# Two loads of v moved from SyncE's DMA queue to ScalarE's, in a sparse-attention and maxout kernel

## The chip, the cores and the metric

One core of one Trainium2 chip. The metric is the device time of one execution in microseconds. The kernel before has a median of 173.41 us (172.84, 173.2 and 173.63, and one slow run of 175.87).

## The reference

```python
batch, n_heads, seq, head_dim = 4, 8, 768, 64        # q, k, v in float32
block, window = 32, 16
k_sum = k.reshape(B, H, nb, block, D).max(axis=3)     # block maxima of k
v_sum = v.reshape(B, H, nb, block, D).mean(axis=3)    # block means of v
# each query sees its window of 2*16-1 keys, and all 24 block maxima (+ log 32)
a = softmax(concat(window scores, block scores))
attn = a @ concat(v, v_sum)
x = attn as (3072, 512)
out = maximum(x @ w1, x @ w2) @ w_out                 # d_ff = 1024
```

The kernel computes the maximum as w1-part plus relu of x times wd, with wd = w2 - w1. The first attention needs k and q of batch 0, then v of batch 0 (two loads of four heads, called the first and the second v below), and the first hidden product needs x of that attention and wd.

## The kernel before: the parts concerned

Each engine's instruction order, and the landing slot of each load, are fixed by a list (S is SyncE, A ScalarE, D VectorE, G GpSimd, P TensorE; the number is the task, the digit behind the colon a slot).

```python
ORDER = (
    "D3 S38:0,0 D6:0 S40:1,0 D1 D0 ... A92:0 S13:0 G5:0 A101:1 "
    "S14:4 P103:0,0 A93:2 ... A96:1,0 G32:0,0 S41:0 D68:3 D11:0 P70:4,0 S16:5 "   # S14, S16: the two loads of v of batch 0
    "D97:0 P95:0 A77:1 D72:0,0 S42:6 ... S43:7 D83 D84 P88:2 D106:1 S52:0 "      # S42.. : weights
    "P90:6 A89:0 D15:0,0 P86:4 A91:1 D19 ... D17:0 ...")                         # D15, D17: casts of v
# ... cut ...
land = Ring(tiles("land", 8, [128, 2048], F32))       # eight landing slots for all loads

def load_v(b, prio, gap, on):
    vb, parts = Buf(vbr), [Buf(Ring([None])) for _ in range(2)]
    # ... cut ...
    for n in range(2):
        f = Buf(land)
        view = lambda f=f: f.ap[:, 0:1536].rearrange("p (h m d) -> p h m d", h=4, d=D)
        op("SP", 3.6, lambda view=view, n=n: nc.sync.dma_start(
            out=view().rearrange("p h m d -> p (h m) d"),
            in_=v[b, 4 * n:4 * n + 4].rearrange("h (m r) d -> r (h m) d", r=128)),   # rows of 64 floats = 256 B
           write=[f], behind=v_spread[b - 1], prio=prio + gap * n, label=f"load v{b}{n}")
        copy(on, ...)                                  # the cast of v, on VectorE for b = 0
# ... cut ...
def split_w12(n, fs, prio, prio_t):
    part = slice(256 * (n % 2), 256 * (n % 2) + 256)
    op("DVE", {"DVE": 1.2, "POOL": 2.36}, lambda e: (nc.vector if e == "DVE" else nc.gpsimd).tensor_tensor(
        out=wd[n].ap[:], in0=wide(fs[1])[:, :, part], in1=wide(fs[0])[:, :, part], op=ALU.subtract), ...)
```

The softmax here doesn't subtract the row's maximum and nothing guards it: scores larger than these inputs give would overflow.

## Time and profile before

| | before |
|---|---|
| median, us | 173.41 |
| profiled span, us | 171.9 |
| first hidden matmul (TensorE, line 660) starts, us | 30.74 |
| from there to the end, us | 141.2 |
| VectorE casts the first v / the second v at, us | 16.93 / 20.98 |

The page's main rows and SyncE's issues stand in the prediction. First ScalarE's timeline at the place where the second v will be issued (start us, duration us, engine, line, operation, tiles, and in brackets the idle time before it with what ended it):

```profile
9.25 0.79 ACT L410 COPY kx<-banks 128x768 bf16<-128x768 bf16 x1
10.65 0.83 ACT L410 CAST kqb<-land 128x768 bf16<-128x768 f32 x1 [0.61 <-DMA land<-in_k_dram]
12.08 0.80 ACT L410 COPY kx<-banks 128x768 bf16<-128x768 bf16 x1 [0.60 <-PE banks L434]
```

The last of these, ScalarE's second kx copy, is read by VectorE's third block maximum of k (the "third reduction" below):

```profile
13.91 0.95 DVE L454 TENSOR_REDUCE ks<-kx 128x24 bf16<-128x768 bf16 x1
```

Then GpSimd's and VectorE's timelines between 22 and 31 us:

```profile
23.77 1.20 POOL L410 CAST w1b<-land 128x1024 bf16<-128x1024 f32 x1 [10.06 <-DMA land<-in_moe_w_dram]
26.52 4.86 POOL L607 TENSOR_TENSOR wd<-land,land 128x1024 bf16<-128x1024 f32 x2 [1.55 <-DMA land<-in_moe_w_dram]
```

### The profile page before, as it was taken

Reading aid. Unit: us, or ns where it says so; the run is one execution under the profiler, and the core shown is the slowest. Engines: PE = TensorE matmul, PEld = TensorE weight load, DVE = VectorE, ACT = ScalarE, POOL = GpSimd, SP = SyncE. Lnnn points to the kernel's source line nnn. Section 1 sums busy time; section 2 is a strip of 40 time slices with the busy share of each in tenths; the row PEclk is TensorE's granted clock in tenths of the full one; section 3 lists DMA queues with packets and bytes.
Section 4 is the critical chain, followed back from the end, with each engine's and each line's share of the span. In section 5 each row is a group of like instructions: output and inputs, shape, how many; then the busy total and the mean of one; then the engine's idle time right before and its main releaser. Section 6 shows DMA issues by size and latency. Waiting matters only on the chain.

```text
span 171.9 us, 5167 instructions
## 1 busy us (share of the span) xinstructions
PE 148.1 (86%) x2229; PEld 97.5 (57%) x2256; DVE 114.6 (67%) x208; ACT 89.3 (52%) x120; POOL 41.5 (24%) x61
## 2 busy tenths in 40 slices
PE   0136585999999999899999989999999999999992
PEld 0124354645865575468656745677565558856451
DVE  1279999847767869759898847799896741224031
ACT  3375897756865795348768252567553140231020
POOL 7521028522263002795003375100000000000000
PEclk9999969999999999999999999999999999999999
DMA  4999999999999799999999955720022110000645
GB/s 159 341 293 221 305 388 386 391 373 338 221 281 251 154 270 235 253 312 350 323 263 158 256 169 98 229 77 4 0 89 98 65 61 0 4 0 0 208 158 183
DMA packets 42742, 34.22 MB, mean 199 GB/s; under 512 B 25952, under 2 KB 36704, under 8 KB 42720
## 3 DMA queue, kind: packets, MB, share of 16 engines
q1 hardware_dynamic: 42720, 33.90, 70.0%
q8 instruction: 17, 0.28, 0.7%
q14 instruction: 5, 0.04, 0.1%
HBM read 25.17 MB, written 6.29 MB: 183 GB/s over the span
## 4 chain that ended last, share of the span: by engine, by line
PE 78%; DVE 11%; DMA 4%; issue 2%; ACT 1%; SPq 1%; DVEq 0%
PE banks L660 24%; PE banks L681 24%; PE banks L674 11%; DVE vx L410 4%; PE banks L501 4%; DMA land<-in_k_dram 4%; PE banks L644 4%; PE banks L543 4%; PE banks L434 3%; PE banks L575 2%; DVE ks L454 2%; DVE qx L410 1%; SPq L305 1%; PE banks L346 1%; DVE xs L552 1%
## 5 line engine op out<-in xcount | busy, mean ns | idle before, releaser
L660 PE MATMUL banks<-xt,wd 128*128 128x256 bf16 x384 | 46.6, 273 | 0.0
L681 PE MATMUL banks<-wo,g 128*128 128x512 bf16 (+1 forms) x187 | 44.1, 370 | 1.6 <-issue 1.4
L660 PEld LDWEIGHTS <-wd 128*128 128x128 bf16 x384 | 36.8, 98 | 8.5
L515 ACT ACTIVATE pb<-banks,bias 128x1024 bf16<-128x1024 f32 x24 | 25.8, 1113 | 7.7 <-PE banks L501 7.6
L406 ACT ACTIVATE g<-banks 128x512 bf16<-128x512 f32 x30 | 17.2, 599 | 22.9 <-PE banks L660 22.7
L681 PEld LDWEIGHTS <-g 128*128 128x128 bf16 x200 | 18.3, 98 | 17.0
L410 POOL CAST kqb<-land 128x768 bf16<-128x768 f32 x18 | 16.0, 904 | 42.6 <-DMA land<-in_q_dram 20.2
L674 PE MATMUL banks<-w1o,xt 128*128 128x512 bf16 (+1 forms) x88 | 23.1, 370 | 1.2 <-issue 0.8
L408 DVE TENSOR_SCALAR g<-banks 128x512 bf16<-128x512 f32 x18 | 12.3, 689 | 13.8 <-PE banks L660 13.6
L410 ACT COPY o<-banks 128x512 f32<-128x512 f32 (+1 forms) x15 | 8.6, 571 | 22.8 <-PE banks L681 22.6
L434 PE MATMUL banks<-identity,kqb 64*128 64x64 bf16 x384 | 9.9, 201 | 11.7 <-ACT kqb L410 6.7
L552 DVE TENSOR_TENSOR xs<-banks,inv 128x512 bf16<-128x512 f32 x24 | 16.1, 684 | 0.5
L434 PEld LDWEIGHTS <-kqb 64*128 64x128 bf16 x384 | 7.7, 101 | 15.0 <-ACT kqb L410 6.8
L454 DVE TENSOR_REDUCE ks<-kx 128x24 bf16<-128x768 bf16 x16 | 15.0, 944 | 1.4 <-ACT kx L410 1.2
L674 PEld LDWEIGHTS <-xt 128*128 128x128 bf16 x100 | 9.1, 98 | 7.9
L410 DVE COPY o<-banks 128x512 f32<-128x512 f32 (+1 forms) x10 | 6.6, 663 | 10.3 <-PE banks L681 8.3
L509 DVE TENSOR_TENSOR pb<-pb,mask 128x1024 bf16<-128x1024 bf16 x18 | 13.2, 750 | 0.3 <-ACT pb L515 0.2
L410 ACT COPY qx<-banks 128x768 bf16<-128x768 bf16 x12 | 9.5, 804 | 5.6 <-PE banks L434 2.8
L501 PEld LDWEIGHTS <-kx 64*128 64x128 bf16 x416 | 8.6, 102 | 5.4 <-issue 3.9
L501 PE MATMUL banks<-qx,kx 64*128 64x64 bf16 (+2 forms) x416 | 10.2, 199 | 1.0 <-DVE kx L461 0.5
L543 PEld LDWEIGHTS <-pb 128*64 128x64 bf16 x384 | 7.5, 110 | 6.1 <-issue 4.3
L410 DVE COPY kx<-banks 128x768 bf16<-128x768 bf16 x7 | 6.7, 952 | 6.5 <-PE banks L434 5.5
(63 smaller groups left out, 149.6 us busy)
## 6 DMA issues: line engine op xcount, KB each, us to landing
land<-in_k_dram SPq DMA_DIRECT2D x16, 384.0 KB, 6.9
land<-in_q_dram SPq DMA_DIRECT2D x16, 384.0 KB, 8.2
land<-in_v_dram SPq DMA_DIRECT2D x8, 768.0 KB, 10.4
out_dram<-o SPq DMA_DIRECT2D x19, 256.0 KB, 2.5
land<-in_moe_w_dram SPq DMA_DIRECT2D x4, 1024.0 KB, 10.4
land<-in_moe_w_out_dram SPq DMA_DIRECT2D x2, 1024.0 KB, 14.3
vx<-vb SPq DMA_DIRECT2D x3, 396.0 KB, 7.1
out_dram<-o SPq DMA_DIRECT2D x4, 224.0 KB, 3.4
```

What stands on the lines that cost most here:

```text
L406: nc.scalar.activation(out=o, in_=i, func=ACT.Relu)
L410: {"DVE": nc.vector.tensor_copy, "ACT": nc.scalar.copy, "POOL": nc.gpsimd.tensor_copy, "SP": nc.sync.dma_start}[e](out=o, in_=i)
L434: nc.tensor.transpose(out=bank(ps, 2048, BF16)[:, at:at + 64], in_=src.ap[r, j].rearrange("p h d -> p (h d)"), identity=identity[r, r])
L454: op("DVE", 0.95, lambda: nc.vector.tensor_reduce(out=ks.ap[:].rearrange("p (t s) -> p t s", s=2), in_=kt()[:, :, 0:64].rearrange("p t (s ...
L501: nc.tensor.matmul(**m)
L509: nc.vector.tensor_tensor(out=o, in0=o, in1=m, op=ALU.mult)
L515: op("ACT", 1.13, lambda: nc.scalar.activation(out=pb.ap[:].rearrange("p a n -> p (a n)"), in_=bank(ps, 1024), func=ACT.Exp, bias=bias[:], ...
L543: nc.tensor.matmul(out=av()[64 * par:64 * par + 64, c, 2 * u + a, :], lhsT=pb.ap[:, a, at:at + 64], rhs=vx[b].ap[:, 4 * grp + 2 * u + par, ...
L552: op("DVE", 0.69, lambda: nc.vector.tensor_tensor(out=x.ap[:, grp] if g1 == grp else x.ap[:, grp:g1 + 1, hp % 2], in0=av()[:, :, :, 0:D], ...
L660: nc.tensor.matmul(out=bank(ps)[:, 256 * s:256 * s + 256], lhsT=wd[n].ap[:, c, 128 * s:128 * s + 128], rhs=x_rows(b, grp)[:, c, :], start= ...
L674: nc.tensor.matmul(out=bank(ps, hi - lo), lhsT=x_rows(b, grp)[:, c, sl], rhs=w1o[c].ap[:, lo:hi], start=(c == 0), stop=False)
L681: nc.tensor.matmul(out=bank(ps, hi - lo), lhsT=g.ap[:, f, sl], rhs=wo[f // 2].ap[:, f % 2, lo:hi], start=False, stop=(f == FC - 1))
```

## The change

The intent: with v on a second queue, the q load behind it no longer sits 8.54 us in its issue, weights can be issued earlier, and v travels beside k, q and the weights.

```diff
-            op("SP", 3.6, lambda view=view, n=n: nc.sync.dma_start(
+            op("SP", 3.6, lambda view=view, n=n: (nc.sync if b else nc.scalar).dma_start(
                 out=view().rearrange("p h m d -> p (h m) d"),
                 in_=v[b, 4 * n:4 * n + 4].rearrange("h (m r) d -> r (h m) d", r=128)),
```

## The prediction

> **What bounds the kernel now.** I read the page first. Its 40 slices say that TensorE is busy at 90% or more from the eighth slice on (some 30 us into a span of 171.9 us), and that the DMA engines are full over the same first 30 us:
>
> ```profile
> span 171.9 us, 5167 instructions
> ...
> PE   0136585999999999899999989999999999999992
> ...
> DVE  1279999847767869759898847799896741224031
> ...
> DMA  4999999999999799999999955720022110000645
> ```
>
> So there are two stretches: a start of 30 us in which loads and VectorE prepare the first attention, and 140 us in which TensorE is packed. The chain that ended last, in order of time, agrees: one k load up to 9.53 us, then almost nothing but VectorE pieces to 30 us, then TensorE pieces to the end. A microsecond lost before 30 us therefore moves the end by about a microsecond; there is no later slack to swallow it. One gained counts only if it shortens that VectorE stretch.
>
> Second, the timeline of the start, SyncE's DMA issues (start, duration, what):
>
> ```profile
> 0.82 0.96 SPq L305 DMA_DIRECT2D land<-in_k_dram  x2
> 1.81 0.47 SPq L305 DMA_DIRECT2D land<-in_q_dram  x1
> 2.33 0.98 SPq L305 DMA_DIRECT2D land<-in_k_dram  x2
> 3.35 0.99 SPq L305 DMA_DIRECT2D land<-in_q_dram  x2
> 4.38 0.47 SPq L327 DMA_DIRECT2D land<-in_v_dram  x1
> 4.89 8.54 SPq L305 DMA_DIRECT2D land<-in_q_dram  x1
> ...
> 13.48 0.47 SPq L327 DMA_DIRECT2D land<-in_v_dram  x1
> ```
>
> The q load after the first v sits in its issue for 8.54 us. That is what the change is after. But the queue is not empty meanwhile. The trace's landings (last of 16 parts): first q 8.49 us, third and fourth k 9.51 and 10.57, next q's 11.61 and 12.74, first v 15.42, the blocked q 16.51, second v 19.96, w1 23.72. The engines carry the earlier loads until v is through, with about 1 us of thinner traffic near 13 to 14 us.
>
> Third, what VectorE does with them:
>
> ```profile
> 9.53 0.56 DVE L410 CAST kqb<-land 128x768 bf16<-128x768 f32 x1 [1.90 <-DMA land<-in_k_dram]
> ...
> 16.06 0.95 DVE L454 TENSOR_REDUCE ks<-kx 128x24 bf16<-128x768 bf16 x1
> 16.93 0.95 DVE L410 CAST vb<-land 128x1536 bf16<-128x1536 f32 x1
> 17.98 0.57 DVE L410 COPY vx<-vb 64x1584 bf16<-64x1584 bf16 x1
> 18.58 0.56 DVE L410 CAST kqb<-land 128x768 bf16<-128x768 f32 x1
> ...
> 20.98 0.96 DVE L410 CAST vb<-land 128x1536 bf16<-128x1536 f32 x1
> ```
>
> Only the k cast waits for a DMA, 1.90 us. The v casts start with no wait: VectorE arrives 1.5 us after the first v landed (16.93 against 15.42) and 1.0 us after the second (20.98 against 19.96). In windows of 4.3 us VectorE is busy 4.12, 4.08, 4.21 and 4.07 us from 12.9 to 30. An earlier v is worth nothing there; a v that is over 1 to 1.5 us later, or a later k, costs.
>
> **What the Trainium skill says.** "DMA: Bandwidth & Descriptors", section Issuing engines are not separate DMA queues: the transfers of all issuers run on the same 16 engines and interleave, and a second issuer "will only save the time on the sequencer it takes to initiate the DMA, which is usually small relative to the DMA itself". The trace agrees on one shared resource (full from 2 to 37 us), but here one issue lasts 8.54 us. The same page, Queues, rings and completion order: each DMA engine round-robins between queues at packet granularity, and SP and ACT have a ring of their own on each engine but no descriptor generator of their own. The trace before has one data queue, so it shows nothing of the sharing. It does show that every row of v is a packet of 256 B (3072 a load, 192 per engine), against 1536 B for k and q (16 per engine and load) and 2048 B for the weights (32).
>
> **The change part by part.** The built program shows what moves: TensorE, VectorE and GpSimd keep their order. ScalarE gets the first v behind its second cast (5.24 us) and the second v behind its first kx copy (9.25 us). SyncE loses two issues, and the wo load that followed the third weight load now also waits for the first v to land, through a shared semaphore.
>
> Removed: 8.54 us of SyncE blocking. The last q comes out about a microsecond sooner than 16.51, but VectorE casts it only at 18.58. The weights move ahead of v. Weights are first needed at 23.8 us, and the first hidden matmul at 30.7 waits for VectorE's x, which waits for v. Gain on the path: about 0, at most the 1 us of thin traffic.
>
> Added, first: the share of v. The trace's windows give rates over 16 engines: 352 to 372 GB/s with 1536 B packets, 228 to 239 with 256 B, 388 with 2048 B. Per engine one packet takes 66, 17.5 and 84 ns. If the two queues take turns packet by packet, v gets one small packet per big one: 84 ns a turn beside k and q, 102 ns beside weights, where alone it would take 17.5. First v packets flow about 1.1 us after the issue (0.82 to 1.9 for the first k), so near 6.5 us. I count on the slowest engine, since a load has landed only when it has (first q: 15 parts by 6.2 us, the last at 8.49). At 7.4 us it has six k and q loads left, 96 packets: 96 x 84 ns = 8.1 us, to 15.5. Half of v's 192 packets are through. The other 96 pair with the three weight loads already queued: 96 x 102 ns = 9.8 us, to about 25.3. The first v lands near 25.5 instead of 15.42, and VectorE loses 25.5 - 16.9 = 8.6 us. The second v then runs alone until wo is released (4 us, to 29) or shares with wo and the next weights (up to 40): 8 to 19 us behind its 20.98. These losses overlap, as both are waits of one in-order engine: 8 to 19 us in all.
>
> Added, second: k and q slow down. The third k, the one VectorE waits for, has 32 packets ahead and in it: 32 x 17.5 ns = 0.6 us later, straight on the chain; the fourth 0.8.
>
> Added, third: ScalarE can be blocked as SyncE was. The issue behind a v was accepted about 2 us before that v's last part landed (13.43 against 15.42; 17.38 against 19.96; in the next batch 44.47 against 47.02), so with some 100 packets of v left on the slowest engine. With turns of 84 ns, about 92 packets are gone at 7.4 + 7.7 = 15.1 us. ScalarE would hang in the second v's issue from 9.3 to 15 us, and its k cast (10.65), kx copy and qx copies start 4 to 5 us late. That delay lies inside the wait for v.
>
> Sum in full: 173.2 + 8 to 19, less a little overlap, so 180 to 191.
>
> **The rivals.** (a) Sharing by bytes, not packets: v gets half the rate, some 16 small packets for every 2.7 of k and q. Then v lands before 15 us and ScalarE is hardly held, but the third k is pushed back by up to 3 us, and the whole VectorE chain with it: 174 to 177. For it: the skill's remark that a packet can hold several descriptors. Against: the trace records every 256 B row by itself. (b) The shared generator holds everything behind a full ScalarE ring: the first v still pairs with what is queued, to 20 to 24 us, but the second then has the engines to itself, about 4 us: 178 to 182. (c) Nothing moves: v hardly competes, lands in its 1 to 1.5 us of slack, and VectorE's stretch stays: 173 to 174. For it speaks only that the bytes and the consumers' order are unchanged. (d) Faster: the thin microsecond is saved and small packets hide under big ones, 172 to 173. It can't become 2%, because VectorE is full from 9.5 us on and the first k loads are ahead of v in either version.
>
> **Range and chances.** I give the packet-by-packet case some 45%, (a) 20%, (b) 15%, (c) and (d) 20%. Every case but the last two loses, either at v or at k. The middle of that is about 181 us; 173.0 to 190.0 us should hold it 8 times in 10. Slower by over 2% means over 176.7: all of the first and (b), and a third of (a), some 0.70. Within 2%: 0.28. Faster: 0.02.
>
> **What would show it.** If I'm right: the first v lands past 20 us and the second past 26, VectorE shows a DMA wait of several us before the vb casts, ScalarE has a gap behind its kx copy at about 10 us with a v issue of some 5 us in it, the first hidden matmuls start at 38 us or later instead of 30.7, and from there to the end the time is the same as before (141 us). In (a) the waits stand before the kqb casts instead and v lands early. I'm wrong if v lands by 17 and 21 us with k no later than 10: then packets of two queues do not take turns as I assume, and the time stays.

## More of the kernel before

```profile
23.25 0.22 DVE L461 COPY kx<-ks 128x288 bf16<-128x288 bf16 x1
23.50 2.47 DVE L410 COPY vx<-vb 64x1584 bf16<-64x1584 bf16 x3
26.00 0.97 DVE L410 COPY vx<-vx 32x2904 bf16<-32x2904 bf16 x1
```

VectorE starts the last of its copies within SBUF at 26.00; GpSimd starts its two subtractions for wd at 26.52, when w2 has landed.

## The result, and the profile after

The changed kernel took 185.59 us (185.31 to 186.67, 4 runs) against 173.41: ratio 1.0725, 95% interval 1.0664 to 1.0787, slower. Ratios here and below are the mean time of one kernel's fast runs over that of the other's of the same rounds, so not quite the ratio of the medians quoted.

The page after, the same three rows:

```profile
PE   0110345779999999998999999999999999999993
...
DVE  1280298997658758775799874789897654231221
...
DMA  4999999999981505999999979662004110000455
```

TensorE's dense part begins some 11 us later (slice ten of 4.6 us, before slice eight of 4.3 us). The first hidden matmul starts at 42.50 us instead of 30.74, and from there the span has 141.4 us left, against 141.2. The whole loss, 11.8 us, arises before the first hidden matmul.

SyncE's issues after:

```profile
3.35 2.16 SPq L305 DMA_DIRECT2D land<-in_q_dram  x3
5.56 5.68 SPq L599 DMA_DIRECT2D land<-in_moe_w_dram  x3
25.90 0.92 SPq L629 DMA_DIRECT2D land<-in_moe_w_out_dram  x2
```

The intent is met: no issue of q or weights lasts long (the three weight issues take 0.89, 0.37 and 0.37 us; the rest of the 5.68 us lies between them), and w1 lands at 18.13 us instead of 23.72. (Landings here and below are the trace's, the last of a load's 16 parts.) But the first v lands at 25.75 instead of 15.42 and the second at 28.59 instead of 19.96. The DMA view from 15 to 21 us says why, with its row for each queue:

```profile
DMA packets 1902, 2.13 MB, mean 355 GB/s; under 512 B 981, under 2 KB 981, under 8 KB 1902
## 3 DMA queue, kind: packets, MB, share of 16 engines
q1 hardware_dynamic: 949, 1.89, 89.5%
q10 hardware_dynamic: 953, 0.24, 18.8%
```

q1 is SyncE's queue and q10 ScalarE's. 949 packets and 953: the two queues get equal turns. That these are turns of one packet each shows at the end of the weights, when one engine alone still has some: its last weight packets start evenly, 97 to 110 ns apart (22.92 to 24.16 us), where 2048 B packets alone took 84 ns (the prediction's figure from the kernel before). But a weight packet has 2048 B and a v packet 256 B, so v moves 0.24 MB while the weights move 1.89 MB. Once the weights run out on most engines, at 22 us, v goes about five times faster (843 packets between 22 and 23 us, against 953 in these 6).

ScalarE's timeline shows a second thing:

```profile
8.70 10.88 ACTq L327 DMA_DIRECT2D land<-in_v_dram  x1
9.43 0.79 ACT L410 COPY kx<-banks 128x768 bf16<-128x768 bf16 x1
19.69 0.83 ACT L410 CAST kqb<-land 128x768 bf16<-128x768 f32 x1 [9.46 <-issue]
21.12 0.80 ACT L410 COPY kx<-banks 128x768 bf16<-128x768 bf16 x1 [0.60 <-PE banks L434]
```

The issue of the second v holds ScalarE's instruction stream for 10.88 us, so the k cast behind it starts at 19.69 instead of 10.65. The stall that SyncE had has moved to an engine that computes. It doesn't hold SyncE too: two of SyncE's weight issues, at 9.74 and 10.88 us, fall into this time and take 0.37 us each. VectorE after, and GpSimd's subtractions:

```profile
21.95 0.95 DVE L454 TENSOR_REDUCE ks<-kx 128x24 bf16<-128x768 bf16 x1 [8.41 <-ACT kx L410]
22.82 1.08 DVE L458 COPY kx<-kx 128x32 bf16<-128x32 bf16 x1
23.82 0.94 DVE L410 COPY qx<-banks 128x768 bf16<-128x768 bf16 x1
24.68 1.51 DVE L458 COPY kx<-kx 128x32 bf16<-128x32 bf16 x1
...
27.24 0.95 DVE L410 CAST vb<-land 128x1536 bf16<-128x1536 f32 x1
```

```profile
21.52 4.64 POOL L607 TENSOR_TENSOR wd<-land,land 128x1024 bf16<-128x1024 f32 x2 [2.31 <-DMA land<-in_moe_w_dram]
```

VectorE waits 8.41 us, for ScalarE and not for v: by its cast at 27.24 the first v has been there for 1.5 us. Two copies of 0.17 us each take 1.08 and 1.51 us, 2.25 us more. The reduction and the copy out of the matmul's banks between them (0.95 and 0.94 us) keep their length. GpSimd's subtractions, started early because w2 came early (21.45 us instead of 26.44), run from 21.52 to 26.2. So three suspects: the hold of ScalarE, the late v that may be hidden behind it, and VectorE's copies beside GpSimd.

### The profile page after: what moved, and what is told of

It is laid out like the page before. It is cut to its first block, busy times and chain, and to the rows that moved or that the text cites. A ratio compares the mean times of both kernels' runs of the same rounds, so it can differ in the third digit from the quotient of the medians.

```text
span 183.9 us, 5196 instructions
## 1 busy us (share of the span) xinstructions
PE 152.8 (83%) x2256; PEld 98.7 (54%) x2256; DVE 116.1 (63%) x208; ACT 89.0 (48%) x120; POOL 40.3 (22%) x61
## 3 DMA queue, kind: packets, MB, share of 16 engines
q10 hardware_dynamic: 6176, 1.57, 4.6%
## 4 chain that ended last, share of the span: by engine, by line
PE 77%; DVE 8%; issue 6%; DMA 4%; ACT 2%; SPq 0%; ACTq 0%; DVEq 0%
PE banks L660 24%; PE banks L681 23%; PE banks L674 11%; PE banks L543 4%; DVE vx L410 4%; PE banks L501 4%; PE banks L644 4%; DMA land<-in_q_dram 4%; PE banks L434 3%; PE banks L575 2%; DVE kx L458 1%; DVE qx L410 1%; ACT kqb L410 1%; ACT kx L410 1%; PE banks L618 1%
## 5 line engine op out<-in xcount | busy, mean ns | idle before, releaser
L660 PE MATMUL banks<-xt,wd 128*128 128x256 bf16 x384 | 47.1, 275 | 0.0
L681 PE MATMUL banks<-wo,g 128*128 128x512 bf16 (+1 forms) x200 | 46.7, 372 | 0.0
L410 POOL CAST kqb<-land 128x768 bf16<-128x768 f32 x18 | 14.7, 830 | 50.6 <-DMA land<-in_k_dram 19.8
L674 PE MATMUL banks<-w1o,xt 128*128 128x512 bf16 (+1 forms) x100 | 24.7, 372 | 0.0
L410 ACT CAST kqb<-land 128x768 bf16<-128x768 f32 x9 | 7.5, 832 | 14.4 <-issue 9.5
L509 DVE TENSOR_TENSOR pb<-pb,mask 128x1024 bf16<-128x1024 bf16 x18 | 11.9, 680 | 0.3 <-ACT pb L515 0.2
L543 PEld LDWEIGHTS <-pb 128*64 128x64 bf16 x384 | 8.1, 118 | 6.0 <-issue 4.9
```

The source lines that it names most:

```text
L410: {"DVE": nc.vector.tensor_copy, "ACT": nc.scalar.copy, "POOL": nc.gpsimd.tensor_copy, "SP": nc.sync.dma_start}[e](out=o, in_=i)
L543: nc.tensor.matmul(out=av()[64 * par:64 * par + 64, c, 2 * u + a, :], lhsT=pb.ap[:, a, at:at + 64], rhs=vx[b].ap[:, 4 * grp + 2 * u + par, ...
L660: nc.tensor.matmul(out=bank(ps)[:, 256 * s:256 * s + 256], lhsT=wd[n].ap[:, c, 128 * s:128 * s + 128], rhs=x_rows(b, grp)[:, c, :], start= ...
L674: nc.tensor.matmul(out=bank(ps, hi - lo), lhsT=x_rows(b, grp)[:, c, sl], rhs=w1o[c].ap[:, lo:hi], start=(c == 0), stop=False)
L681: nc.tensor.matmul(out=bank(ps, hi - lo), lhsT=g.ap[:, f, sl], rhs=wo[f // 2].ap[:, f % 2, lo:hi], start=False, stop=(f == FC - 1))
```

## The experiments

Each ran beside the kernel before on its chip; medians in us. The k and q loads land a little differently from run to run: the last of a load's 16 parts trails the fifteenth by up to 2.5 us in the first 15 us. So read a run's waits, not only its absolute times. Starts on VectorE, with the idle time before the step in brackets:

| run | k cast | third reduction | first v cast | second v cast | last vx copy | first hidden |
|---|---|---|---|---|---|---|
| before | 9.53 | 13.91 (0.11) | 16.93 (0) | 20.98 (0.03) | 26.00 | 30.74 |
| after | 9.75 | 21.95 (8.41) | 27.24 (0) | 31.59 (0.03) | 37.21 | 42.50 |
| second v later | 8.36 | 12.25 (0.11) | 24.74 (9.39) | 28.89 (0.03) | 33.94 | 39.65 |
| hold alone | 7.95 | 19.46 (7.26) | 22.48 (0) | 31.21 (0.03) | 37.15 | 41.95 |
| first v only | 8.86 | 12.76 (0.11) | 19.34 (3.48) | 23.44 (0.03) | 33.49 | 38.79 |
| second v only | 9.17 | 13.53 (0.11) | 18.70 (2.07) | 22.92 (0.03) | 32.16 | 37.46 |
| no subtraction, before | 8.02 | 12.39 (0.11) | 15.41 (0) | 19.76 (0.03) | 24.79 | 30.18 |
| no subtraction, first v only | 9.70 | 13.60 (0.11) | 19.66 (2.95) | 24.42 (0.03) | 28.70 | 34.39 |
| GpSimd's queue | 8.42 | 12.63 (0.11) | 17.53 (1.80) | 23.66 (2.00) | 33.71 | 39.00 |

**The late v without the hold.** The change, with the second v's issue moved behind ScalarE's first exp:

```diff
- "... D11:0 P70:4,0 S16:5 D97:0 ... D15:0,0 P86:4 A91:1 ..."
+ "... D11:0 P70:4,0 D97:0 ... D15:0,0 S16:5 P86:4 A91:1 ..."
```

> Both v loads stay on ScalarE's queue beside the weights, but the second is issued later, behind ScalarE's first exp, so that ScalarE's k cast, kx and qx copies are not held (its lane needs no wait). Theory 'both': the turns with the weights alone cost nearly as much as the hold: the first v still lands near 25.5 us (25.75 after the change), the k cast on ScalarE starts near 10.7 instead of 19.7, and VectorE now shows a DMA wait of 7 to 9 us ahead of its first vb cast. Time 181 to 185 us. Rival 'hold only': ScalarE's 10.9 us in one issue is the whole loss and the late v is no loss by itself: 173 to 176 us.

Measured: 183.2 us against 173.72, ratio 1.0543 (1.0485 to 1.0601). ScalarE's k cast is at 9.42; the first v lands at 24.71; VectorE:

```profile
14.40 0.95 DVE L454 TENSOR_REDUCE ks<-kx 128x24 bf16<-128x768 bf16 x1
24.74 0.96 DVE L410 CAST vb<-land 128x1536 bf16<-128x1536 f32 x1 [9.39 <-DMA land<-in_v_dram]
```

The late v, which the profile after doesn't show as a wait at all, costs most of the loss by itself. "Hold only" falls. (The second v's issue still holds ScalarE here, for 4.03 us from 14.96 on, but VectorE's wait, 15.35 to 24.74, covers it.)

**The hold without the late v.** The kernel before, with nine copies of a scratch tile on ScalarE where the change issues the second v:

```diff
-            op("SP", 3.6, lambda view=view, n=n: nc.sync.dma_start(...), ...
+            def issue(view=view, n=n):
+                nc.sync.dma_start(...)
+                if b == 0 and n == 1:
+                    for _ in range(9):
+                        nc.scalar.copy(out=idle_out[:], in_=idle_in[:])      # 128x1024 bf16
+            op("SP", 3.6, issue, ...
```

> The kernel before, all loads on SyncE's queue, with nine copies of a 128x1024 scratch tile put on ScalarE where the changed kernel issues the second v (about 9.4 us of ScalarE, as long as the hold). v lands as before (15.4 and 20.0), later weights may move a little. Theory 'both': 8 to 10 us on the end, 181 to 184 us, with VectorE idle some 8 us before its third k reduction, although v is there. Rival 'late v only': the held copies have slack, and the time stays under 176.

Measured: 184.85 us, ratio 1.0659 (1.0586 to 1.0733). The copies hold ScalarE for 9.66 us (7.64 to 17.30), v lands at 14.67 and 19.33, and VectorE idles 7.26 us before its third reduction. "Late v only" falls too. Alone they cost 5.4% and 6.6%, both together 7.25%: they lie side by side in time and don't add up. But the 6.6% hold more than the hold. A large part of this run's loss lies between the first and the second v cast (8.7 us against 4.05 before), and is of the third kind, VectorE's copies beside GpSimd:

```profile
25.11 2.32 DVE L466 COPY kx<-kx 128x32 bf16<-128x32 bf16 x1
27.34 0.56 DVE L418 COPY vx<-vb 64x1584 bf16<-64x1584 bf16 x1
27.91 3.02 DVE L418 COPY vx<-vx 32x2904 bf16<-32x2904 bf16 x1
```

A copy of 0.17 us takes 2.32 and one of 0.97 takes 3.02, while GpSimd's two subtractions run from 24.8 to 30.1.

**One load at a time.** Only the first v on ScalarE's queue (`nc.sync if b or n else nc.scalar`), then only the second (`nc.scalar if not b and n else nc.sync`). Neither has a DMA behind it on ScalarE, so there is no hold.

> Only the first v on ScalarE's queue; the second stays on SyncE's behind the last q and ahead of the weights. ScalarE has nothing behind its one DMA, so no hold. The first v takes turns with k and q and then with the 256 B packets of the second v, which are short: it lands at 18 to 20 us, the second near 21. VectorE waits 1 to 3 us for the first v. Time 174 to 177 us. If turns cost by time on the queue and not by packet size, the first v would land as late as after the change (25 us) and the time would be over 180.

> Only the second v on ScalarE's queue, issued behind its first kx copy; the first stays on SyncE's ahead of the last q. ScalarE is not held (its one DMA is the first on its queue). The two v loads take turns with each other: the first v lands at 18 to 20 us instead of 15.4, the second near 19 to 21. VectorE waits 1 to 3 us for the first. Time 174 to 177 us; the other outcome, no loss at all (172 to 174), if the first v, ahead in its ring, is hardly slowed.

Measured: 182.09 us against 174.47, ratio 1.0442 (1.0397 to 1.0487), and 181.83, ratio 1.0341 (1.0263 to 1.042). Two of the four runs with the second v only were slow, so its loss is read from the ratio: some 5.9 us. The landings came as expected (19.32 and 20.09; 18.67 and 20.35), and the waits for the first v nearly so (3.48 and 2.07 us). The times did not: 7.6 and 5.9 us lost where 1 to 3 were expected. The loss comes after both casts. VectorE and GpSimd in the run with the first v only:

```profile
24.32 1.07 DVE L461 COPY kx<-ks 128x288 bf16<-128x288 bf16 x1
25.31 0.16 DVE L458 COPY kx<-kx 128x32 bf16<-128x32 bf16 x1
25.48 1.14 DVE L410 COPY vx<-vb 32x1320 bf16<-32x1320 bf16 x2
26.54 2.37 DVE L461 COPY kx<-ks 128x288 bf16<-128x288 bf16 x1
28.94 4.52 DVE L410 COPY vx<-vb 64x1584 bf16<-64x1584 bf16 x3
```

```profile
23.63 1.67 POOL L410 CAST w1b<-land 128x1024 bf16<-128x1024 f32 x1 [10.21 <-DMA land<-in_moe_w_dram]
26.36 4.78 POOL L607 TENSOR_TENSOR wd<-land,land 128x1024 bf16<-128x1024 f32 x2 [1.06 <-DMA land<-in_moe_w_dram]
```

The weights land when they did before, so GpSimd subtracts from 26.36 on as before. VectorE is 2.5 us later than before, and its last copies meet the subtractions. A copy of 0.22 us takes 2.37: it runs from 26.54 to 28.91, and the subtraction that it meets from 26.36 to 28.83. The page "SBUF — State Buffer" of the Trainium skill, section Who interferes with whom, says that VectorE's copies and casts can take a port pair that GpSimd also uses, that whoever issues first holds it for the whole instruction, and that the other "fully blocks". The times here agree with that: the blocked copy ends 0.08 us after the subtraction, and after the change the two copies of 1.08 and 1.51 us end 0.03 us after a subtraction each. GpSimd's casts do the same on a smaller scale: even in the kernel before, one of VectorE's copies took 1.31 us instead of 0.57 (24.08 to 25.39) beside the w1b cast (23.77 to 24.97).

**The subtractions taken away.** GpSimd's two subtractions cut to two columns (the result is wrong), in the kernel before and in the one with the first v only:

```diff
-            out=wd[n].ap[:], in0=wide(fs[1])[:, :, part], in1=wide(fs[0])[:, :, part], op=ALU.subtract),
+            out=wd[n].ap[:, :, 0:width], in0=wide(fs[1])[:, :, cut], in1=wide(fs[0])[:, :, cut], op=ALU.subtract)
+   # width = 2 on GpSimd, 256 on VectorE; wd[0], wd[1] set to zero at the start
```

> Wrong on purpose: the kernel before with GpSimd's two wd subtractions (2.4 to 2.5 us each, 26.5 to 31.4 us) cut to two columns, the rest of wd set to zero at the start. It is the base of the next run. VectorE's copies between the second v cast and the last vx copy are already ahead of the subtractions before, so they take 5 us as before (5.17) and the time stays at 172 to 174.5 us.

> Wrong on purpose in the same way: only the first v on ScalarE's queue, without GpSimd's subtractions. Theory 'collision': of the 7.6 us that the first-v-only run lost, some 2.4 are the wait for v and some 5 are VectorE's copies running beside GpSimd's subtractions (10.2 us of copies instead of 5.2). Without them the copies take 5 to 6.2 us (GpSimd's w1b cast is still there), and the time is 2 to 3.5 us over the run without subtractions before: 174.5 to 177. Rival: the copies are slow for another reason (the DMA traffic of two queues): they stay near 10 us and the time near 181.

Measured: 174.04 us (ratio 1.0019, 0.9989 to 1.0049) and 176.95 us (ratio 1.0189, 1.0158 to 1.0221), against 173.77; the second is unclear at the 2% mark. The subtractions are free in the kernel before, and cost the first-v-only kernel about 5 us: it loses 2.9 us to its own base without them, 7.6 with them. Its copies are back to their own length:

```profile
26.69 0.22 DVE L463 COPY kx<-ks 128x288 bf16<-128x288 bf16 x1
26.94 1.73 DVE L412 COPY vx<-vb 64x1584 bf16<-64x1584 bf16 x3
```

The rival, that two queues' DMA traffic slows the copies, falls: from 23 to 31 us the traffic is the same in both runs (386 and 389 GB/s), and by then all of it is on SyncE's queue. The same removal was not done for the other runs; there the copies' times beside GpSimd's speak for the same cause.

**No weights beside v.** The first weight load put into the first v's slot, so that SyncE can't issue weights while that v is in the way; once with the second v at the change's place, once behind the first exp. I built this pair twice.

```diff
- S42:6 S43:7 S52:0 ... S53:4
+ S42:4 S43:7 S52:0 ... S53:6      # first form; the second form also moves S42, S43, S52 behind D15
```

> The changed kernel with the first weight load put into the first v's landing slot, so that SyncE issues no weights until VectorE has cast that v. v on ScalarE's queue then takes turns with k and q only. Expected: first v lands at 17 to 18 us, ScalarE is held in the second issue only until about 15 us (some 5 us of hold past 10 us instead of 9.5), loss at the end 3 to 5 us: 176 to 179 us. If the hold had nothing to do with the turns (a fixed cost of a second issue on ScalarE), it would stay near 10.9 us and the time near 183.

> Both edits at once: second v issued behind the first exp, and the weights held until the first v is cast. Neither a hold nor weight turns are left. Theory 'both': within 2% of before, 173 to 176 us, first v landing at 17 to 18. If a third cost is at work (the second queue by itself), it stays above 178.

> The mended form of the run with the weights held (there the weights overwrote the first v before it was cast, so the result was wrong and VectorE waited for weights). Now the first weight load goes to the first v's landing slot and is issued after VectorE's cast of it; both v on ScalarE's queue at the places of the change. v takes turns with k and q only: first v lands near 16 to 17, ScalarE's second issue takes about 6 us (6.08 in the failed form, 10.88 after the change). Loss at the third reduction 2 to 4 us, and, if copies then meet GpSimd's work, up to 5 more. 176 to 181 us. The theory falls if ScalarE is held as long as after the change.

> The mended form of both edits: weights behind the first v's cast, and the second v issued behind ScalarE's first exp, when the first v is through. No hold and no turns with weights are left, though the same two loads are on ScalarE's queue. First v near 16.5, second near 20.5, as before. 173 to 175.5 us, within 1% of before. If the second queue costs something by itself, it stays over 177.

All four gave wrong results, at 186.4, 187.6, 184.79 and 184.82 us (ratios 1.0734, 1.0779, 1.0606, 1.0612; the second one's profile is of a slow run). In the first form the weights overwrote the first v before its cast. In the second form the swapped slot of the last weight load is taken again by a later load before wd is made from it: VectorE's subtractions for wd wait 6.1 and 5.6 us for q. So the end times say nothing on the theory, and the expectations for them are not met. The stretch up to the second v's cast is sound in the second form, and there is one reading to take from each. With the second v at the change's place:

```profile
7.46 6.23 ACTq L327 DMA_DIRECT2D land<-in_v_dram  x1
8.19 0.79 ACT L410 COPY kx<-banks 128x768 bf16<-128x768 bf16 x1
13.79 0.83 ACT L410 CAST kqb<-land 128x768 bf16<-128x768 f32 x1 [4.81 <-issue]
```

The issue takes 6.23 us instead of 10.88, and the first v lands at 16.33: without weights in the turns the hold is 4.65 us shorter, so it is no fixed cost of a second issue. That the 6.23 us that stay belong to the turns with k and q and to v's late start is argued, not tested apart. With the second v behind the first exp, v lands at 15.88 and 21.43, and VectorE casts the first without waiting and the second after 1.08 us:

```profile
16.23 0.95 DVE L410 CAST vb<-land 128x1536 bf16<-128x1536 f32 x1
...
21.46 0.96 DVE L410 CAST vb<-land 128x1536 bf16<-128x1536 f32 x1 [1.08 <-DMA land<-in_v_dram]
```

So the second queue by itself doesn't make the first v late; the second is 1.5 us later than before, as it was issued only at 15.83. That the end would then be back at 173 us is not shown.

**SyncE's blocked issue, without a second queue.** The last q ahead of the first v on SyncE (`S41:0` moved ahead of `S14:4`).

> The kernel before with one swap in SyncE's order: the last q ahead of the first v, so that no k or q stands behind a v. No second queue. The 8.54 us in the q's issue go to the second v's issue, the last q lands near 14 instead of 16.5, the first v near 16.5, and nothing on VectorE's path is earlier: 172.5 to 174.5 us, same. If SyncE's blocked issue had been worth anything it would be faster by over 1 us.

Measured: 173.48 us against 174.47, ratio 0.996 (0.9918 to 1.0002): the same. The last q lands at 12.15 instead of 16.51, and the long issue moves to the second v (7.46 us). So a q that isn't blocked is worth nothing. The block itself stands in SyncE's queue still. That earlier weights would gain nothing shows in the kernel before without subtractions: there wd was ready at 26.2 us instead of 31.4, and the time was the same.

**GpSimd's queue instead of ScalarE's** (`nc.sync if b else nc.gpsimd`).

> Both v loads issued on GpSimd instead of ScalarE, at the same places in the program. ScalarE is free. If a queue is served packet by packet whoever fills it, the first v again lands past 20 us beside the weights and VectorE waits for it: 180 to 186 us, with GpSimd perhaps held in its issue (its kqb casts at 11.8 late). If GpSimd's queue is served otherwise (larger packets), v lands before 18 us and the time is 173 to 176.

Measured: 182.43 us, ratio 1.045 (1.04 to 1.05). The time is in the range, the reason is the other one. The DMA view from 12 to 20 us:

```profile
DMA packets 707, 2.10 MB, mean 263 GB/s; under 512 B 20, under 2 KB 23, under 8 KB 706
## 3 DMA queue, kind: packets, MB, share of 16 engines
q0 software_dynamic: 349, 1.36, 64.7%
q1 hardware_dynamic: 357, 0.72, 39.8%
```

Turns again, 349 to 357, but GpSimd's packets hold 1.36 MB / 349 = 3.9 KB each, some fifteen rows of v. Now v takes two thirds of the bytes, lands at 17.51 and 23.64, and w1 at 23.83, as in the kernel before (23.72), not at 18.13 as after the change. GpSimd's two issues take 1.57 and 1.45 us, so it is not held. VectorE waits 1.80 and 2.00 us, then meets the subtractions like the one-load runs: copies of 2.37 and 4.51 us again. The page "DMA: Bandwidth & Descriptors", section SWDGE vs HWDGE vs iDMA, gives up to 4096 B as the preferred packet of GpSimd's queue; this run agrees.

No version beat the kernel before, so there is none to recommend; q_first is equal to it within 1%.

## Why the prediction was right or wrong

The direction and the range held (some 181 forecast, 173.0 to 190.0, measured 185.59); the loss was 12.2 us where 181 stands for 7.6. The main mechanism, turns by packets, is right. The path by which the loss reached VectorE is another than forecast, and that the sum of the main case (180 to 191) still holds the result is in part luck: hold and blocked copies made up what was put down to waits for v.

- **No gain from the freed issue**: right. Weights 5.6 us earlier shortened nothing, a wd ready 5.2 us earlier (the kernel before without subtractions) neither, and an unblocked q was worth nothing in the q_first run.
- **Turns packet by packet**: right, 949 to 953 packets. Predicted landing of the first v 25.5 us, measured 25.75; of the second "to 29" or "up to 40", measured 28.59. That 25.5 is so close is luck in part: v started 1.6 us later than assumed, when fewer k and q were left, so that the slowest engine had time for some 150 turns with large packets and not 192 (an estimate: 9.02 to 24.16 us at 100 ns). The rivals of sharing by bytes and of v not competing are out, and so is the cause named in (b): SyncE's issues went on while ScalarE was held.
- **k and q slowed by 0.6 to 0.8 us**: not seen. The third k landed at 9.73, 0.2 later than before and inside its spread over the runs (7.8 to 9.7), and no v packet moved before 9.0 us. I had put the first at 6.5, by the 1.1 us from issue to first packet of the very first load; here it took 3.9 us (5.16 to 9.02).
- **ScalarE held from 9.3 to 15 us**: right in kind, mis-sized. The term measured 10.88 us, 8.70 to 19.58. All three factors were too small: v's first packet came at 9.02 and not 7.4; by the acceptance 106 of v's 192 packets per engine had started (1699 in all), not 92; and a turn took 99.5 ns (16 engines over 161 v packets a us), not 84.
- **"That delay lies inside the wait for v"**: the step that failed. It was the other way round: VectorE waited 8.41 us for ScalarE and not at all for v, so the sign I gave, a DMA wait of several us before the vb casts, did not appear. It appeared, 9.39 us, when the hold was taken away. The working names ScalarE's late kx copy but doesn't follow it to VectorE's third reduction, which needs it and stands ahead of the v cast; its reading of the chain as "almost nothing but VectorE pieces" also passes over 3.6 us of TensorE and ScalarE between 16.08 and 19.71. Two delays of nearly one length lay side by side. By the hold alone VectorE would have come to the first v's cast at 25.0 us (an estimate: 27.24 less the 2.25 of the blocked copies), 0.8 before v landed; the blocked copies took that last bit of the wait away.
- **VectorE's stretch shifts as a block**: a silent assumption, and wrong. Its copies within SBUF are blocked by GpSimd's instructions when they meet. After the change this is 2.25 us of the 11.8 ahead of the first v's cast (and about 0.6 behind the second's, beside GpSimd's wo casts); in the run with the first v only it is 4.7 of 7.6. So a v that is only 2 or 3 us past its slack cost several us more than the lateness, which the prediction doesn't have.
- **Then the same to the end**: right, 141.4 us against 141.2.
- **The chances**: by the shares given, "slower" adds up to 0.67 (0.45, 0.15 and a third of 0.20), not 0.70.

Still open: why ScalarE's first v packet came 3.9 us after its issue (3.9 to 4.3 in all runs with a v on ScalarE's queue early), and whether removing hold and turns together restores 173 us.

## What to carry to other kernels

Before you move a load to a second queue, compare its packet size with that of the loads it will meet: turns by packets give a load of short rows a small share, and an issue behind such a load can hold the engine that makes it (8.54 us on SyncE, 10.88 on ScalarE here), so keep a second DMA away from an engine with work to do. A wait that a profile doesn't show may only be hidden behind another one, so take one suspect away at a time. And an engine whose copies run just ahead of a neighbour's work on a shared port has little slack there, even where no wait is shown.

## What the Trainium skill lacked or had wrong

- "DMA: Bandwidth & Descriptors", section Issuing engines are not separate DMA queues, says that a second issuer saves the sequencer's issue time, "usually small". Here the time was 8.54 us on SyncE and became 10.88 us on ScalarE; the page lacks that an issue behind a load with many packets holds the issuing engine until over half of that load has started, and no page gives a size for it. Counted from the packet records, the issue behind a first v was accepted when 106 of its 192 packets per engine had started after the change, 98 in the run with the second v later, 131 with the weights held back, and 180 in the kernel before: no constant number.
- The same page, section Queues, rings and completion order, states turns at packet granularity, with 9 to 17 descriptors as a typical packet. Turns are confirmed (949 to 953, one packet each on the last engine), but on SyncE's and ScalarE's queues each 256 B row was recorded as a packet of its own; the page doesn't draw the consequence for unequal rows (0.24 MB against 1.89 MB in 6 us).
- The same page gives some 0.6 us to the first byte on these queues; here it was 1.1 us from the first issue of all, and 3.9 to 4.3 us for a v on ScalarE's queue while the engines were full. I found the latter in no page.
- "SBUF — State Buffer", section Who interferes with whom, was right on the lock, so nothing to mend there: copies of 0.17 and 0.22 us took 2.32 and 2.37 and ended within 0.1 us of the end of the subtraction that they met.
